# A fused agent-attention and SoLU feed-forward kernel: the same work in another order on its five queues

## The chip, the core and the metric

The kernel runs on one core of a Trainium2 chip. The core has a matrix engine (TensorE, PE in the profile; PEld is its weight load), a vector engine (VectorE, DVE), a scalar engine (ScalarE, ACT), a general engine (GpSimd, POOL) and SyncE (SP), which here does nothing but issue transfers. Each works through its own instruction stream in order; semaphores hold an instruction until what it needs is there. The metric is device time in microseconds (us) of one execution, lower is better.

## What is computed

Cut to what matters, the reference is:

```python
scale = 1.0 / np.sqrt(128)
def sm(a, b):                                   # B = 4 batches
    s = scale * (a @ b.transpose(0, 2, 1))
    e = np.exp(s - s.max(-1, keepdims=True))
    return e / (e.sum(-1, keepdims=True) + 1e-09)
agent_v = sm(agents, k) @ v                     # 49 agents, 12608 keys per batch
x = (sm(q, agents) @ agent_v).reshape(50432, 128)
h = x @ w_in                                    # 128 -> 1024
e = np.exp(h - h.max(-1, keepdims=True))
solu = h * e / (e.sum(-1, keepdims=True) + 1e-09)
ln = (solu - mean(solu)) / sqrt(var(solu) + 1e-06) * g_ln
out = ln @ w_out                                # 1024 -> 128
```

All inputs and the output are float32.

## The kernel before

The 50432 tokens are cut into 394 tiles x of 128 tokens. Three kinds of work are interleaved.

**Phase A** (`phase_a`, once per batch b) makes the batch's small matrix from K and V: 12 blocks of 1024 keys and a short last one. `kload` (L581) and `vload` (L587, and L592 for the short block's pieces) issue loads of 512 KB each; then come scores on PE (L598), maximum on DVE (L603, L610), exponential on ACT (L624), transposes on PE (L631), their copy (L641) and the product with V on PE (L651), added up on DVE (L660). Its end is a chain of small steps, among them `f1` (PE L707, the batch's agent_v), `f2` (L710, ACT copies it to `av_dup`), `q1` (DVE L714, its largest value) and the product with w_in (L741), whose result stays in SBUF as `mh` and `ml`, float16 halves. Batch 0's phase A stands at the head of the program; that of batch b+1 is spread between the tiles of batch b, and the last batch's tiles have none beside them.

**Phase B** (`phase_b`, once per unit of 8 tiles) loads q (`qload`, L841, 512 KB), makes the second softmax's weights (PE L859, DVE L865 and L870, ACT L874, casts L879 on ACT or L881 on POOL, L885) and turns them by a transfer that transposes (`b5`, L889, into `pT`).

**The tile's own steps.** PE makes h (`c_h`, L951, into `ph`, two buffers). DVE scales it and takes the extreme (`c_max`, L967, into `e_a` or `e_b`), ACT takes the exponential (`c_exp`, L974), DVE multiplies (`c_u`, L982, into `u`, six buffers), ACT squares for the variance (`c_sq`, L1003). For 343 of the 394 tiles u is split into two float16 parts (`c_f0`, L990 on POOL or L988 on ACT; `c_f1`, L993 on POOL; `f`, five buffers), and a transfer transposes both parts (`c_x`, L997 on SP, into `x`, eight buffers); the other 51 are transposed on PE (L1010). Then PE multiplies by w_out (`c_w`, L1031). Per 16 tiles the row factors are made (`c_rstd`), and per group of 4 tiles `c_fin` (DVE L1078, into `ob_a` or `ob_b`) scales the sums and `c_out` (SP L1082) stores 256 KB. `c_fin` of group g writes the buffer that the store of group g-2 reads.

**What sets the order.** The kernel lists all its steps with their dependencies (`op`), and a table of numbers, `STEPS`, gives the order in which `Plan.run` hands them out and, for steps that two engines can do, which of them does it:

```python
for i, k in todo:          # todo = steps(), unpacked from STEPS
    o = self.ops[i]
    e = o.eng[k]
```

Nothing else decides: each engine's stream, SP's among them, holds its steps in the order of this table. Steps wait for their inputs and for buffers to come free, and nothing overtakes on an engine. The times that `Plan` adds up beside this choose which of four PSUM banks a step takes, and put some filling matmuls (L1092) into PE's idle time in the head.

Of the kernel before, what the change touches and what calls it, by code (L numbers as in the profile page):

```python
# [30 lines left out]
    "B?AgPvJ2V=60J8EZT`fz$-AeSQO$h#)5lj%G<bVHZSsz{-}?4YxWFD%_l2LF10zned`jA*?$HG{o8*0-^78|qD-3!LfVD(s+yTQWr?GZ^`3w*Z"
    "jm{ZI60D4f49m%#2(}EDqnR;uXikS0g7f#78*7OguS>_`D%=H(86UnX0p$ad@rZYqs0!f|*M6n16^%59_a?T~yBZZb-ZrP~O|FgN34K(tDC^iO"
    "zgDi*D&5<=ohI*Uh01Hyt-CAHaJ(a`Jhqp4zWr4bs`3v7V<4TX(Q7T2p_PC%3glkX&;3erWqa=0dw}bWE5?;zTpp3{y2U$-y$YW`)*I`(=-LiM"
    "mcS4H)fzt9-qN1L9p{>z-oahJW9#^~Ryh`PtoCdg&XvjA=DE0|b9Z{;ZrPOFGI^&49I4?+h4|hzj9p@pW}`N!s@%5WO@m8d?qK81zCsf10+(1|"
    "Y3;nRRWj?fY4^`mD>AGaG}U{4^F#3KzotEwfW7$SB}QPW6ke+x-#Kd<U26~H$`f-P_~_e?(<(eY=EKmKucHHK_8K47@W`}1yi<J*H`0P`f92m9"
    "tv!eHmL}rV)!zn&7BdbV-qEQVw-NfmYBymDjWzeiq@vQpo3k;E-V{*Sw$O{ZgLZ%#2HV!p^kC?JkS={x8k1Xmhw{LdT|bBZ+Hcezw%MK58Tp2K"
    "#aKFF?>$@|xU)OUZ>zQSj)C!tDTlXj(BJJV)g9XJB*RjjTvq{R!HD+o&1@hvF>Nc?*GwMB?<>dg<>~dorOv9YMgO-x)q6ZIRhV{h`L$SebgC%r"
    "@n6+UG%jzYu(Q2jP!^~<nO`6}Ce$Kx<KTTl4v3@_Pn?;+&6%<qq;x*Rl7A)^x0o72RlP`M9P<f>H^W1C^lWM7&LG?G*f}4Kq8q(4<*swg{bQe%"
    "Oj~dnK<5JqFTUbg0}Ya2{<1sXC0{sJjp5S4$UYiUl%30ff2cYDErN|{<7fJS8ueSE*k1457X^nqb#EfAmA0>Z6vOt00Q?ukG!K&ag4L<}+_(2M"
    "Da*RYbkck)mV$%k+k@)%w2!bXL>CrB>5MUL-oPfo@Pd6pJd_qKDNl!8|LYgVmBZfpQ(K~9V58-5Y^(&7znM?m>lPL<Apk?Nkx)nfENXtRjaLjR"  # L40
    "S4a2jwVP7ilEgAlwbhN@RHa3-^MCPsfB2!k-zdT2LCa<1p}5gJSPe2rEHa#wnY*>|tukfBimLL`*K{_Lkj28{ChTkfFfFt9`A37Q)be<&q8y+T"
    "oh<`~3fWl$x~@Brc$$@p8I9Cy`p<vq?P@nt&H+3&7%xpd;+u+5XLDQzR`Au?Giz7{WampW4Kv=YDU011wT*ap4$oA3s<nDWxKfpB3B^_&vormx"
    "p*u<Y!mxHHT<fSGAasZ4sfrS?8gpD$40%!DP3YFm^Z)1Xnmr?P130d6bjwonolVzM3!=#>%^o2=Zob;tU*B4&@*F7=O&6>34?bCQa@I$fyTx6X"
    "m{E4Nt@GkdU>i4st&46nB6ry%n=O5WBe8gmiB6h)h7wf|s>F2RgZ5b6;V_8!>f3EDsn*#Zlh0dB>8(u_Ix+olq*`dx>>Q27#j<smx9Z|h5BEN^"
    "w|C`l^iRY;^^M(;3f&N9{ki{UK!kWZIBSSTPL}<8FgiP`MWaNbO|_qtJI7AvkLOi*2SBI9O?U!7mac+*NdTy#`U$DKcD8es7y=KD>9sy-OXzZI"
# [36 lines left out]
    "Hi2eJKJ^Wcx#`PaQwdK>M!;Ex1PH}dQH+o#amC;KIQXf5b*Q<&N8%O7-5#Ut=1L}AtrW_z_(hqr4A|`DF*ypB+Rw1Fk^a@S;lnno5jg+pUzUs7"
# [1194 lines left out]
```

## Time and profile before

| | us |
|---|---|
| Median of 3 runs | 1303.37 |
| Lowest and highest run | 1299.05 and 1303.8 |
| The profiled execution, its own time | 1300.81 |
| Span of the profiled execution (first to last instruction) | 1299.0 |

A profile gives, for one execution, when each engine was busy and what ended each idle stretch before an instruction. Read it by stage: a mean over the program mixes the head (batch 0's phase A), the long middle (tiles with the next batch's phase A beside them, to about 990 us), the last batch's tiles (990 to 1274) and the tail. A transfer has three times: when SP issues it, how long SP is held by that (the duration in SP's rows, marked SPq), and when it lands (to landing).

### The profile page before, as it was taken

The numbers are of one execution on the slowest core, as the hardware profiler recorded it, in microseconds if no ns is written. First come the engines' busy times: TensorE is split into PE (matmuls) and PEld (weight loads), VectorE is DVE, ScalarE is ACT, GpSimd is POOL, SyncE is SP. The second block draws the span as 40 slices with busy tenths as digits, with TensorE's granted clock in tenths as the row PEclk, the third lists the DMA queues.
The fourth block names the chain that finished last, engine by engine and source line by source line (L and its number), as shares of the span: only waits on it lengthen the run. The fifth ranks groups of instructions, "written<-read, shape, count | busy, mean of one in ns | idle before, by whom it ended". The sixth has DMA issues, their size and how long they took to land.

```text
span 1299.0 us, 36435 instructions
## 1 busy us (share of the span) xinstructions
PE 1204.2 (93%) x14305; PEld 916.7 (71%) x14305; DVE 1177.5 (91%) x2127; ACT 1174.8 (90%) x2157; POOL 1131.2 (87%) x910
## 2 busy tenths in 40 slices
PE   7889988999999888998989998989998999999998
PEld 4566766777777666776767776767776777776777
DVE  6899888989999888998979997988997999999997
ACT  5599888999999888998979998988997999999998
POOL 3589788899999987979988897988997999999996
PEclk9999999999999999999999999999998999999999
DMA  9699999999999999999999999999998999999988
GB/s 371 194 250 237 240 228 222 242 232 229 222 229 246 235 241 249 237 242 235 222 225 227 243 241 229 236 245 250 247 222 167 230 236 218 208 222 208 213 208 181
DMA packets 805484, 300.62 MB, mean 231 GB/s; under 512 B 770496, under 2 KB 774080, under 8 KB 805312
## 3 DMA queue, kind: packets, MB, share of 16 engines
q1 hardware_dynamic: 805312, 298.30, 108.8%
q8 instruction: 112, 1.84, 0.6%
q14 instruction: 60, 0.49, 0.1%
HBM read 79.67 MB, written 25.82 MB: 81 GB/s over the span
## 4 chain that ended last, share of the span: by engine, by line
ACT 30%; DMA 16%; PE 15%; POOL 13%; DVE 13%; issue 12%; SPq 1%; DVEq 0%; POOLq 0%; ACTq 0%
ACT ph L974 13%; ACT sq L1003 12%; PE px L1031 6%; PE ph L951 4%; DVE e_b L967 2%; POOL f_c L993 2%; POOL f_b L993 2%; DVE e_a L967 2%; POOL f_e L993 2%; DMA x_f<-f_d 2%; PE px L651 2%; DMA out_dram<-ob_a 1%; POOL f_a L993 1%; POOL f_d L993 1%; DVE u_a L982 1%
## 5 line engine op out<-in xcount | busy, mean ns | idle before, releaser
L974 ACT ACTIVATE ph<-e_a,nm 128x1024 f32<-128x1024 f32 x197 | 218.6, 1109 | 30.1 <-DVE e_a L967 28.9
L974 ACT ACTIVATE ph<-e_b,nm 128x1024 f32<-128x1024 f32 x197 | 218.5, 1109 | 14.9 <-DVE e_b L967 14.4
L951 PE MATMUL ph<-mh,pT_a 128*128 128x512 f16 x264 | 102.4, 388 | 12.5 <-DVE u_a L982 3.4
L951 PE MATMUL ph<-mh,pT_b 128*128 128x512 f16 x260 | 99.3, 382 | 13.2 <-DVE u_e L982 6.6
L951 PE MATMUL ph<-mh,pT_c 128*128 128x512 f16 x260 | 99.2, 382 | 11.0 <-DVE u_c L982 4.5
L951 PE MATMUL ph<-ml,pT_a 128*128 128x512 f16 x264 | 102.0, 387 | 0.1
L951 PE MATMUL ph<-ml,pT_b 128*128 128x512 f16 x260 | 99.4, 382 | 0.0
L951 PE MATMUL ph<-ml,pT_c 128*128 128x512 f16 x260 | 99.4, 382 | 0.0
L982 DVE SCALAR_TENSOR_TENSOR u_a<-e_a,cb,ph 128x1024 f32<-128x1024 f32 x66 | 84.2, 1276 | 5.4 <-ACT ph L974 4.4
L982 DVE SCALAR_TENSOR_TENSOR u_c<-e_a,cb,ph 128x1024 f32<-128x1024 f32 x65 | 82.9, 1275 | 4.0 <-ACT ph L974 3.3
L982 DVE SCALAR_TENSOR_TENSOR u_d<-e_b,cb,ph 128x1024 f32<-128x1024 f32 x66 | 84.2, 1276 | 2.5 <-ACT ph L974 2.1
L982 DVE SCALAR_TENSOR_TENSOR u_e<-e_a,cb,ph 128x1024 f32<-128x1024 f32 x65 | 82.9, 1275 | 2.8 <-ACT ph L974 1.8
L982 DVE SCALAR_TENSOR_TENSOR u_b<-e_b,cb,ph 128x1024 f32<-128x1024 f32 x65 | 82.8, 1274 | 2.7 <-ACT ph L974 2.2
L982 DVE SCALAR_TENSOR_TENSOR u_f<-e_b,cb,ph 128x1024 f32<-128x1024 f32 x65 | 82.9, 1275 | 2.4 <-ACT ph L974 1.6
L951 PEld LDWEIGHTS <-pT_a 128*128 128x128 f16 x528 | 47.9, 99 | 48.3 <-issue 21.1
L951 PEld LDWEIGHTS <-pT_b 128*128 128x128 f16 x520 | 47.3, 98 | 48.5 <-issue 20.5
L951 PEld LDWEIGHTS <-pT_c 128*128 128x128 f16 x520 | 46.8, 98 | 46.2 <-issue 17.6
L1031 PE MATMUL px<-wh,x_f 128*128 128x128 f16 x688 | 73.0, 221 | 5.1 <-DMA x_f<-f_d 2.2
L1031 PEld LDWEIGHTS <-x_a 128*128 128x128 f16 x1032 | 64.0, 99 | 18.9 <-DMA x_a<-f_b 3.4
L1031 PE MATMUL px<-wh,x_a 128*128 128x128 f16 x688 | 73.4, 221 | 4.0 <-DMA x_a<-f_b 2.4
L1031 PEld LDWEIGHTS <-x_f 128*128 128x128 f16 x1032 | 63.9, 99 | 18.1 <-DMA x_f<-f_d 2.4
L1031 PE MATMUL px<-wh,x_e 128*128 128x128 f16 x688 | 72.5, 219 | 3.9 <-DMA x_e<-f_c 1.3
(472 smaller groups left out, 4842.5 us busy)
## 6 DMA issues: line engine op xcount, KB each, us to landing
out_dram<-ob_a SPq DMA_DIRECT2D x49, 256.0 KB, 2.8
out_dram<-ob_b SPq DMA_DIRECT2D x49, 256.0 KB, 2.8
qt_a<-in_qT_dram SPq DMA_DIRECT2D x24, 512.0 KB, 5.1
qt_b<-in_qT_dram SPq DMA_DIRECT2D x24, 512.0 KB, 5.1
kt_b<-in_kT_dram SPq DMA_DIRECT2D x18, 512.0 KB, 5.1
vt_b<-in_v_dram SPq DMA_DIRECT2D x18, 512.0 KB, 5.8
kt_a<-in_kT_dram SPq DMA_DIRECT2D x18, 512.0 KB, 4.9
vt_a<-in_v_dram SPq DMA_DIRECT2D x18, 512.0 KB, 5.3
```

The source lines that it names most:

```text
L651: nc.tensor.matmul(px[h * AP2 : (h + 1) * AP2, :C], eT[:w, o + h * AP2 : o + (h + 1) * AP2], vt[:w, t, :], start=all(z[0] != h for z in mm ...
L951: nc.tensor.matmul(ph[:, sl], w, m[:, sl], start=(q == 0), stop=(q == len(mm) - 1))
L967: nc.vector.tensor_scalar(out=nhs[x], in0=phs[x], scalar1=nkr[k % 4][:, j : j + 1], scalar2=None, op0=ALU.mult, op1=ALU.min, accum_out=nms[x])
L974: nc.scalar.activation(out=phs[x], in_=nhs[x], func=AF.Exp, scale=-1.0, bias=nms[x], accum_out=rs_[R]["S"][:, j : j + 1])
L982: nc.vector.scalar_tensor_tensor(out=u, in0=nhs[x], scalar=scal(x)[:, 4:5], in1=phs[x], op0=ALU.mult, op1=ALU.mult, accum_out=su)
L993: nc.gpsimd.tensor_tensor(out=fs[x][:, 1, :], in0=us[x][0], in1=fs[x][:, 0, :], op=ALU.subtract)
L1003: nc.scalar.activation(out=sq, in_=u, func=AF.Square, bias=su, scale=-float(DF), accum_out=rs_[R]["Q"][:, j : j + 1])
L1031: nc.tensor.matmul(po, ut, wt[:, kf, :], start=(q == 0), stop=(q == len(mm) - 1))
```

## The change

Only the table `STEPS` differs. Steps, dependencies, buffers and transfers are the same; the order of the steps on every queue is another one, and some steps that two engines can do go to the other engine. The change is described as planning the order anew, with measured mean transfer times and with late landings told by PE's instruction number. The new orders differ from the old nearly everywhere, by a few places.

```diff
--- before.py
+++ after.py
@@ -23,129 +23,129 @@
 STEPS = (
-    "c-pOb4^V1tdf(v{y<9%y7<$T_&vmS^#!!|J<G99J$8}xGu!dU48p2xE5Mmi)EaMu+5^AlnhOmTK;~K|WYKbw_u+|u3T-UI~_!&d2>l%jevDO%C"
...
+    "c-pOb4NxoVdEV+nM~ACRC{Z`+nlPsf!CbDa%2>seU_ywZ5P~r#m=J{!LS+r5l*m+76pg|Vie;jzDv=4M3}L83RSm`rLkU(?MO9=CA><6ERF-vh"
...
 )
```

Engine choices, counted in the built programs: the cast of phase B on ACT (L879) 24 before and 19 now, on POOL (L881) 28 and 33; the small product L913 on ACT 25 and 20, L915 on POOL 29 and 34; the copy L641 on ACT 49 and 47, on DVE 3 and 5; the 1024-column cast on ACT (L988) 64 and 67, on POOL (L990) 279 and 276; four small copies on POOL (L897), two of which are now on ACT (L895). The filling matmuls L1092 are 38 and 46.

Three places of the order follow. In all three, letters count the buffers of a ring, and numbers behind a name count tiles of the program.

**SP, around tiles 242 to 244.** L997 is the transpose of a tile's two halves, L581 and L587 load K and V, L841 loads q, L1082 stores a group, L889 is phase B's transpose. Before:

```order
L1082 DMA out_dram<-ob_b 128x512
L997 DMA_TRANSPOSE x_d<-f_b 128x16x128
L997 DMA_TRANSPOSE x_e<-f_c 128x16x128
L581 DMA kt_a<-in_kT_dram 128x1024
L1082 DMA out_dram<-ob_a 128x512
L587 DMA vt_b<-in_v_dram 128x1024
L587 DMA vt_a<-in_v_dram 128x1024
L997 DMA_TRANSPOSE x_f<-f_d 128x16x128
L581 DMA kt_b<-in_kT_dram 128x1024
L997 DMA_TRANSPOSE x_g<-f_e 128x16x128
```

Now:

```order
L997 DMA_TRANSPOSE x_c<-f_a 128x16x128
L841 DMA qt_a<-in_qT_dram 128x1024
L581 DMA kt_b<-in_kT_dram 128x1024
L889 DMA_TRANSPOSE pT_b<-pack_a 128x8x128
L1082 DMA out_dram<-ob_a 128x512
L581 DMA kt_a<-in_kT_dram 128x1024
L587 DMA vt_b<-in_v_dram 128x1024
L997 DMA_TRANSPOSE x_d<-f_b 128x16x128
L997 DMA_TRANSPOSE x_e<-f_c 128x16x128
L997 DMA_TRANSPOSE x_f<-f_d 128x16x128
L997 DMA_TRANSPOSE x_g<-f_e 128x16x128
```

Four transfers stood in a row ahead of the transpose into x_f; now six stand ahead of the one into x_d, two tiles earlier, and none ahead of x_f.

**ACT, at the end of the last batch's phase A (tiles 284 to 287).** L710 copies `av_dup`, on which DVE's L714 waits; L974 and L1003 are the tiles' exponentials and squares, L988 and L1015 a cast and a copy. DVE has L714 behind the L967 of tile 287 in both orders. Before:

```order
L1015 COPY t_d<-px_169 128x512
L974 ACTIVATE ph_166,S_13131<-e_a,nm_13388 128x1024
L974 ACTIVATE ph_167,S_13131<-e_b,nm_13396 128x1024
L988 CAST f_e<-u_d 128x1024
L1003 ACTIVATE sq_13451,Q_13132<-u_d,su_f 128x1024
L1003 ACTIVATE sq_13454,Q_13132<-u_c,su_e 128x1024
L710 COPY av_dup<-px_170 128x128
L974 ACTIVATE ph_166,S_13131<-e_a,nm_13470 128x1024
```

Now:

```order
L974 ACTIVATE ph_167,S_13152<-e_b,nm_13319 128x1024
L1003 ACTIVATE sq_13368,Q_13153<-u_a,su_c 128x1024
L1003 ACTIVATE sq_13382,Q_13153<-u_c,su_e 128x1024
L1003 ACTIVATE sq_13396,Q_13153<-u_e,su_a 128x1024
L974 ACTIVATE ph_166,S_13152<-e_a,nm_13398 128x1024
L1015 COPY t_d<-px_171 128x512
L710 COPY av_dup<-px_169 128x128
L974 ACTIVATE ph_167,S_13152<-e_b,nm_13417 128x1024
```

The copy L710 stood behind the exponential of tile 287, a cast and two squares; now it stands behind the exponential of tile 286 and a copy, ahead of the exponential of tile 287.

**DVE, at the groups 30 to 32.** L1078 is `c_fin`; the third one in these rows writes `ob_a` again and waits for the store of the first. Before:

```order
L1078 TENSOR_TENSOR ob_a<-px_169,yc_6654 128x512
L1078 TENSOR_TENSOR ob_b<-px_170,yc_6654 128x512
L967 TENSOR_SCALAR e_b,nm_6777<-ph_167,nk_c 128x1024
L982 SCALAR_TENSOR_TENSOR u_a,su_c<-e_a,cb_4311,ph_166 128x1024
L603 TENSOR_REDUCE mxp_5240<-px_169 128x1
L982 SCALAR_TENSOR_TENSOR u_b,su_d<-e_b,cb_4311,ph_167 128x1024
L967 TENSOR_SCALAR e_a,nm_6845<-ph_166,nk_c 128x1024
L1078 TENSOR_TENSOR ob_a<-px_171,yc_6654 128x512
```

Now, from the same place:

```order
L1078 TENSOR_TENSOR ob_a<-px_171,yc_6665 128x512
L1078 TENSOR_TENSOR ob_b<-px_170,yc_6665 128x512
L967 TENSOR_SCALAR e_b,nm_6801<-ph_167,nk_c 128x1024
L982 SCALAR_TENSOR_TENSOR u_a,su_c<-e_a,cb_4312,ph_166 128x1024
L603 TENSOR_REDUCE mxp_5340<-px_170 128x1
L982 SCALAR_TENSOR_TENSOR u_b,su_d<-e_b,cb_4312,ph_167 128x1024
L610 TENSOR_SCALAR nmp_5341<-mxp_5340,nmp_5341 128x1
L967 TENSOR_SCALAR e_a,nm_6848<-ph_166,nk_c 128x1024
L603 TENSOR_REDUCE mxp_5340<-px_171 128x1
L967 TENSOR_SCALAR e_b,nm_6879<-ph_167,nk_c 128x1024
L982 SCALAR_TENSOR_TENSOR u_c,su_e<-e_a,cb_4312,ph_166 128x1024
L610 TENSOR_SCALAR nmp_5341<-mxp_5340,nmp_5341 128x1
```

Between the second and the third L1078 stood five instructions; now sixteen stand there, and the third comes six rows below the end of this piece.

## Rows read from the trace of the kernel before

**Rows 1.** The page, part 1: busy us of each engine (share of the span) and instructions.

```profile
PE 1204.2 (93%) x14305; PEld 916.7 (71%) x14305; DVE 1177.5 (91%) x2127; ACT 1174.8 (90%) x2157; POOL 1131.2 (87%) x910
```

**Rows 2.** Windows: stretch, us, busy us (instructions) by engine, granted clock, DMA share, GB/s.

```profile
78.00:990.00 912.00, 850.29 (x10151) 649.13 (x10150) 824.13 (x1481) 828.51 (x1527) 805.18 (x635) 0.98 1.14 235
990.00:1274.00 284.00, 268.98 (x3271) 209.87 (x3270) 277.46 (x476) 279.43 (x494) 273.60 (x211) 1.00 1.05 213
```

**Rows 3.** Line L967 (DVE): its engine sat idle before it (us, times) until:

```profile
  PE ph L951: 43.9, 55
```

**Rows 4.** Line L997 (the transposes): who waited for it (us, times), and landing.

```profile
  PE px L1031: 26.2, 30
DMA to landing us min/median/max: 3.6/4.7/11.2
```

**Rows 5.** Line L997 in 990 to 1274, where the view names nobody who waited.

```profile
DMA to landing us min/median/max: 3.6/4.2/8.0
```

**Rows 6.** Timeline of SP around 858: start us, us held, queue, line, transfer.

```profile
856.31 0.53 SPq L581 DMA_DIRECT2D kt_a<-in_kT_dram  x1
856.90 0.42 SPq L1082 DMA_DIRECT2D out_dram<-ob_a  x1
857.37 0.42 SPq L587 DMA_DIRECT2D vt_b<-in_v_dram  x1
857.89 0.43 SPq L587 DMA_DIRECT2D vt_a<-in_v_dram  x1
858.42 5.89 SPq L997 DMA_TRANSPOSE x_f<-f_d  x1
```

**Rows 7.** The chain that ended last, 858 to 870: start us, us, what.

```profile
858.42 9.48 DMA x_f<-f_d
...
868.80 1.66 PE ph L951 x4
```

**Rows 8.** Timeline of DVE at its three longest waits for PE; idle before in brackets.

```profile
293.00 1.28 DVE L967 TENSOR_SCALAR_CACHE_REDUCE e_b<-ph,nk_a 128x1024 f32<-128x1024 f32 x1 [3.86 <-PE ph L951]
...
799.54 1.28 DVE L967 TENSOR_SCALAR_CACHE_REDUCE e_a<-ph,nk_c 128x1024 f32<-128x1024 f32 x1 [6.04 <-PE ph L951]
...
870.49 1.28 DVE L967 TENSOR_SCALAR_CACHE_REDUCE e_a<-ph,nk_a 128x1024 f32<-128x1024 f32 x1 [3.06 <-PE ph L951]
```

**Rows 9.** The page, part 3: the queue of instruction loads: packets, MB, share.

```profile
q8 instruction: 112, 1.84, 0.6%
```

**Rows 10.** DMA view of 1105.7 to 1113.8: packets by queue; issue and us to landing.

```profile
q8 instruction: 1, 0.02, 0.8%
...
x_e<-f_e SPq DMA_TRANSPOSE x1, 8.0
```

**Rows 11.** DMA view of 1113.9 to 1118.0, no instruction load in it; us to landing.

```profile
x_g<-f_b SPq DMA_TRANSPOSE x1, 4.0
```

**Rows 12.** Timelines of DVE and ACT, 979 to 985, end of the last phase A.

```profile
984.34 0.29 DVE L714 TENSOR_REDUCE pk<-px 128x1 f32<-128x128 f32 x1 [4.81 <-ACT av_dup L710]
...
980.71 1.03 ACT L988 CAST f_e<-u_d 128x1024 f16<-128x1024 f32 x1
981.64 1.14 ACT L1003 ACTIVATE sq<-u_d,su_f 128x1024 bf16<-128x1024 f32 x1
...
984.06 0.24 ACT L710 COPY av_dup<-px 128x128 f32<-128x128 f32 x1
```

**Rows 13.** Timeline of DVE at the end of the phase A before that one.

```profile
657.07 0.29 DVE L714 TENSOR_REDUCE pk<-px 128x1 f32<-128x128 f32 x1 [1.32 <-ACT av_dup L710]
```

**Rows 14.** Timeline of DVE: four `c_fin` that waited for a store.

```profile
208.74 0.69 DVE L1078 TENSOR_TENSOR ob_a<-px,yc 128x512 f32<-128x512 f32 x1 [4.52 <-DMA out_dram<-ob_a]
...
508.62 0.69 DVE L1078 TENSOR_TENSOR ob_a<-px,yc 128x512 f32<-128x512 f32 x1 [3.52 <-DMA out_dram<-ob_a]
...
669.46 0.69 DVE L1078 TENSOR_TENSOR ob_a<-px,yc 128x512 f32<-128x512 f32 x1 [3.36 <-DMA out_dram<-ob_a]
...
886.25 0.69 DVE L1078 TENSOR_TENSOR ob_b<-px,yc 128x512 f32<-128x512 f32 x1 [2.15 <-DMA out_dram<-ob_b]
```

More of the change, by code (lines that the diff above doesn't have):

```diff
@@ L31 @@
[L31 to L45, printed above, removed]
@@ L146 @@
[L146 to L148 removed]
+    "c-pOb4NxoVdEV+nM~ACRC{Z`+nlPsf!CbDa%2>seU_ywZ5P~r#m=J{!LS+r5l*m+76pg|Vie;jzDv=4M3}L83RSm`rLkU(?MO9=CA><6ERF-vh"
+    "DJ6suWrG!&5)OwSvD<HdB<)JLai$qStaiWse%|kWpXYtvPkGppl#Pt(qf+_O-lfXk&=&%i$|I>FwcdQJI;>ZoHZH#!81LIqg;YUwcKf<avZ-2c"
@@ new lines @@
+    "J5sMnMv`E&SF)iTcb8e^^OI89qPaeFsaZ!sW%8zUrLXjaXuNJ)SEjD7DsBCVj_XKwuvog^5%F3guh8wu$YD?NX1c2MqUoX^wd?A89djk{Q`{lh"
+    "+VI!zR$5gjLkA5z7scAwHI?oQ_kL-x?`+<(Q`(bC*6x&UDYS+Ow9H#u?b7Zvp#z@XMN{3S!4s2%pt{eQTpugnYX&`AqI7rltWenQ9atNm8zoL9"
+    "Xi5(7<ay;KCc)yVYHataQ69licm2`8rD91p(=El^SUDlZoY$kWq-4CuBNkq*U@=10Qj;*rv3@5O-KjrJRP6oEdnt#_)rcP&v8c?viS!PlnAugb"
+    "jmt4v>f4_S|Kyj){``+z%Qtc?sP<Hh#`cE&o_f7$C8V0H83coy#mXZOY7csy0pH@3>7Re?wz4NR)?i%_Z8Q{P8}31SqB1Zh)i(_4K{SZlqG0y$"
+    "_~6wtZo9Pjj%s4-1Hbit$If7FGp53&MsQYj<nCFLn-bUK7>bp489k1Vem8{v(obq@)5=&?kEOF?O;+hY8?oC#yMMZVXYe>uRaKo@!1vZtgI>4a"
@@ new lines @@
+    "o5DOUuW0w&wOZchM2T{Z^2mf<$3{|TSL&n6MN32-N5A!jc1IlPv)4QKfKxQqk+Nd;&f48mE&e;7>zg}wg>lW$>a0?=Ha6KhI{#ar?+s%9y~&Wi"
+    "bl;*Mz-8d0Uy53Fa)Wf}^~lHm``};yP*1mIv&pNQv4Y#gj0;6mXNhJTrbRnzXNO7#BugW&CLE^WqxRcb%fj{b;C4^h>e(wzWu#VuhAS)go3<DH"
+    "b0K5bX;KnLx+bkBHT$)oUE+-D&SD8?tmb5@Ejr?>j#>i&C0YfxiJlWI)_A1|j{U*^(dZ6^rT%$Lrf8T7M`n(fW<%rAV0C@}n)GOG05k3=i(R#$"
+    "sOu2SZbx;vx6*}n?Z{)7a`4~Iem#Y^%mue}X1oQ6rvr0`>bNZ6-Vvv5LlKv|?56a%7OanIEj3}&>$U!P^SlZSL_#u;+HH*9>HL_!vv*<a7%L0+"
+    "0MMqx%N1>_L&+PgM6{)|TKbkA%EyRF5t@>MiOc5IgQVo<x4)oEZ_Z)*2{5H5TJ`9Z{$WY49X?1@jO}+`yn65-OoMG{T}5ZdP|1PJF!AcPWXtQW"
@@ new lines @@
+    "m>C-I6({hdUTdzN=t$$Q0NCg&OH_DOcOpetc3BLTv_JA)bgeP{@am!XpkZm`RKNakeBOzwmKuaaM1HCK>ZeXyary4S(JC631ve`@-Ri)h57_Nt"
+    ")IGQ{8OMxmYV=B@9F#3tn)i-zM@6l)z6K=w)psLWlj<_krk;~)oYi2{c5sc?qFPte{xL2m;#-wA$KWNVOt;S8ouD1fD+^<-%Qe?65i}{i>-HbF"
+    "tu}9(G&WGR*SoAuElwsMijSkclKtlMk^aC68ftOfA_E@x{zCtXc&cY(Qh!yO1mG{eX1H5STc@Xwl#|ZU#iUhtFcleEoxJwihQ=p4mBr48OQKw|"
+    "DkN76$thsD3gS^?#q8*MPw?mdvS%<^KC*t*_vas9x=Yrj$Cg0LVM@KbRVOdDn&hFD)7rC#JMrSqAO6ES%k-^JaeH{D_cou@_rF@6X>N@mA(d(F"
+    "+SgsaSkY95&J8ByXw<n9J!(kUeOtn=xXTb#)E-M?GalDCG=;xCyzMfMjC;eaChWo)M+x_gqe`BX6OK+fKH~y&<LHnMtLZ7T`1)gV$IR7=2=i=R"
@@ L149 @@
+    ")RB1"
 )
```

212 lines of the change are left out of this document (105 added, 107 removed).

## The prediction, made before the changed kernel ran

> **What bounds the kernel now.** I read the page's busy times first [rows 1]: no engine is full, and four lie within 73 us of each other, PE, DVE, ACT and POOL, all between 1131.2 and 1204.2 us of a span of 1299.0. Such a mean hides stages, so next come the windows [rows 2]. In 990 to 1274, where no phase A runs, DVE is busy 277.46 of 284 us (97.7%), ACT 279.43 and POOL 273.60: that stage is full, and no order makes it shorter. In 78 to 990 DVE is busy 824.13 of 912 us (90.4%), so 88 us are idle there. Were it as full as the last stage, it would last 824.13/0.977 = 843.6 us; 68 us are the most that an order could bring. The next view is what ended DVE's idle time. Its dearest entry is L967, waiting for the h tile of PE's L951: 43.9 us in 55 waits [rows 3]. PE in turn waits for the transposes of L997: 26.2 us in 30 times [rows 4], and none of it lies in 990 to 1274 [rows 5]. The landings differ there: the slowest of the program takes 11.2 us, that of the last stage 8.0.
>
> The timeline of SP and the chain of waits, read at 858, show how one goes to the other. Four transfers of K, V and output go out ahead of the transpose into x_f [rows 6]. It lands 9.48 us after its issue, not the median 4.7 [rows 4, 7]; PE stands until then, makes L1031 and then the h tile, and DVE starts at 870.49 after 3.06 us of waiting [rows 7, 8]. Direct transfers ahead of a transpose on SP make it late: of the 15 transposes with four or more others since the one before, 13 landed over 7 us after issue (rows 7 have one); of the 191 with none between, no one did. A second pattern follows PE's instruction number. The program loads its instructions in 112 pieces of 16 KB [rows 9], some 255 PE instructions apart, and a transpose in flight beside one landed after 8.0 us, one shortly after it, with none beside it, after 4.0 [rows 10, 11].
>
> **The change, part by part.** The sum is made against the profiled execution, 1300.81 us (span 1299.0, 1.8 around it); the median of the runs is 1303.37, 2.6 above it, and the forecast is shifted by that.
>
> *Engine choices.* Five casts of phase B, five small products and three 1024-column casts or so change engine; each is one instruction, the wide cast 1.03 us on ACT [rows 12]. Three of these more on ACT are +3.1, and the small ones that leave it give that back; against 1174.8 and 1131.2 us of busy time this is nothing by itself [rows 1]. Taken at 0; bounds -3 and +3, three wide casts either way. The head and tail keep their steps, with some neighbours swapped; no row prices that. Taken at 0 too, with one wait of the size of rows 8, 4 us, either way for the range.
>
> *End of phase A.* DVE's L714 waits for ACT's copy L710. At the last batch DVE stood 4.81 us, since ACT had a cast and two squares ahead of the copy [rows 12]. Now L710 stands behind the exponential of tile 286 and a copy, ahead of that of tile 287. I take 0.8 of waiting to be left, so -4.0 (its far end -4.8). At the end of the phase A before that the wait was 1.32 [rows 13]; there L710 now stands behind two squares, a cast and an exponential, while DVE has two tile instructions to do meanwhile: the same four on ACT are some 4.4 us at 1.03 to 1.14 each, DVE's two some 2.5 at 1.28, so 2 to 2.5 us of waiting, +1.0. The first boundary: 0. Together **-3.0**, bounds -4.8 and +1.
>
> *Stores.* `c_fin` writes the buffer that the store of two groups earlier reads, and four times it waited long [rows 14]. Of these, the one at 508.62 (3.52 us) has now sixteen DVE instructions ahead of it where it had five, and the one at 886.25 (2.15) has 16 us of DVE's work where it had 11: both go, -5.7. Those at 208.74 and 669.46 keep the same tight order or a tighter one: they stay. Two others (groups 28 and 52) come closer, from 11.9 and 8.5 us of DVE's work to 5.0, about as close as the four that waited. I put them together at half of what the four cost on the mean (3.39 each), +3. Net **-2.7**, bounds -5.7 (no new wait) and +5 (both wait in full, and one old one stays).
>
> *Late transposes.* This is the largest term. What tells is how many other transfers stand on SP between two transposes. At the 6.04 us wait, 799.54 [rows 8], the transposes that PE awaited (tiles 222 to 227) had three and four ahead; now none and one: -6.0. At the 3.86 us wait (tile 62) five stood ahead and now one at most, with three ahead of tile 60: half of it, -1.9. At 3.06 (tiles 242 to 244) the crowd of four gives place to one of six, two tiles earlier: 0. Against this the new order has more crowds: 40 transposes with three or more transfers ahead where there were 33, of these 19 with four or more where there were 15. All 43.9 us of L967's waits [rows 3], put on 33 crowds, are 1.3 each; seven more are +9 at most. I take +4, since not all those waits come from crowds, and transposes with nothing ahead went from 191 to 209. Net **-3.9**. Bounds: if nearly all of PE's 26.2 us go [rows 4], less the +4, -22; if four of the seven cost what the three of rows 8 do on the mean, 4.3, +17.
>
> The load of instructions follows PE's number, which an order can count ahead. I found no more cover for the transposes in the new order on the whole: between a transpose's issue and its first use PE has about the same work, a little less. So no gain is added for that.
>
> Here a rule of the Trainium skill bears: the page "Runtime: NRT & Kernel Launch", section "Instruction fetch mechanics", says that a block of instructions is refilled by 16 KiB, that crossing costs one DMA bump and that straight-line code hides most of it. The loads' size agrees with the trace, 1.84 MB in 112 [rows 9]; that it is hidden does not hold for a transpose in flight, 8.0 against 4.0 us [rows 10, 11]. If it were hidden, knowing PE's number would bring nothing, which is one reason for the first rival below.
>
> The sum: 0 - 3.0 - 2.7 - 3.9 = **-9.6**; 1300.8 - 9.6 = 1291.2 for a profiled execution, 1303.4 - 9.6 = **1293.8** for the median.
>
> **Rivals.** *The late landings fall elsewhere* (about the same). Transfers and bytes are the same, and counts of crowds are like before. If each old wait is replaced by a new one as long, the last term is 0 and -3.0 - 2.7 = -5.7 are left: 1297.7; if the stores and the copy are covered by other waits too, 1303. For it: the waits are many and short (55 for 43.9 us), so that two places are a small part [rows 3]. Here belongs also that the change does not do what it says: the order counts PE's instructions, fillers included (38 and now 46), and late landings shift as soon as one wait comes out otherwise.
>
> *More crowds, more waits* (slower). Mechanism: K, V and q loads issued in rows, up to seven together, ahead of a transpose that PE needs at once, as at 858 [rows 6, 7]. Four of the seven added crowds at 4.3 us are +17; with the -5.7 that is +11.3: 1314.7. It decides from three such places on, if no old wait goes (3 x 4.3 = 13, less 5.7, +7). For it: 33 and 40; the six in a row at tile 243. Against: a row of direct transfers sent together leaves the transposes behind it free, and those with none ahead rose by 18.
>
> *The waits really go* (much faster): crowds now stand only where x is ahead by several tiles, so PE's waits for transposes, 26.2 us, nearly all go [rows 4]: -22 and the half of -5.7, since DVE then comes sooner to the stores, -25 in all at the most, and some 1281 when ACT and POOL, at 828.51 and 805.18 of 912 us, begin to be waited for [rows 2].
>
> **How the numbers follow.** Forecast .38, late landings elsewhere .28, more crowds .22, waits really go .12. About 0.5% (6.5 us) is what a measurement of this kernel can tell from no change, so faster means under 1296.9, slower over 1309.9. Faster: .31 of the forecast's .38, all of .12, .03 of the first rival: .46. Slower: .18 of the crowds' .22, .04 of the first rival, .02 of the forecast: .24. Left: .30. The forecast's own range is 1286 to 1300; to hold 8 in 10 it must take in most of the two ends: 1278 to 1316.
>
> **What would show it.** In the profile of the changed kernel: L714's wait at the last end of phase A under 1.5 us, at the one before about 2; no `c_fin` wait at groups 32 and 61; no wait of DVE over 3 us at tiles 222 to 227; L967's waits for PE between 30 and 45 us; the window behind 990 within 2 us of 284, all change lying before it. Wrong would be: a stage before 990 that is longer while L714's and the stores' waits went (then the crowds decide, and PE's waits for L997 exceed 26.2 us), or L967's waits under 25 (then the order does hide the landings, and I have overlooked how).

## The result, and the profile after

The changed kernel takes **1291.46 us**, the median of 5 runs (1288.25 to 1293.5), against 1303.37 for 5 runs of the kernel before: a ratio of 0.9916, with a 95% interval of 0.9889 to 0.9942. The forecast was 1293.8. The profiled execution has a span of 1286.5 us, 12.5 less than that of before; it was the fastest of the five, 3.2 us under their median, as the profiled one of before lay 2.6 under its own.

The page's busy times and the windows, to be held against [rows 1, 2]:

```profile
PE 1192.2 (93%) x14313; PEld 908.2 (71%) x14313; DVE 1175.9 (91%) x2129; ACT 1173.4 (91%) x2150; POOL 1129.7 (88%) x915
```

```profile
78.00:990.00 912.00, 851.56 (x10307) 650.15 (x10306) 838.32 (x1512) 836.45 (x1537) 812.44 (x648) 1.00 1.15 237
990.00:1274.00 284.00, 267.91 (x3274) 209.21 (x3272) 274.44 (x466) 280.61 (x495) 275.87 (x213) 1.00 1.08 215
```

The work is the same: DVE is busy 1175.9 us where it was 1177.5. Its idle time fell from 1299.0 - 1177.5 = 121.5 to 1286.5 - 1175.9 = 110.6 us, by 10.9, and that is nearly the whole 12.5. In 78 to 990 DVE is now busy 838.32 of 912 us, 91.9% instead of 90.4%. The last stage begins some 12 us sooner now, so its own window is 978 to 1261: it is as full as before (97.1%, where it was 97.7%). So the gain lies where the forecast had it, ahead of the last batch's tiles.

```profile
978.00:1261.00 283.00, 267.08 (x3257) 207.03 (x3255) 274.74 (x475) 279.17 (x494) 276.19 (x214) 1.00 1.08 215
```

What ended DVE's idle time in the changed kernel: ahead of L967, of L982, of L1078 and of L714 (one fence for each line's view; us, times).

```profile
  PE ph L951: 29.5, 27
```

```profile
  ACT ph L974: 20.3, 51
```

```profile
  DMA out_dram<-ob_a: 11.3, 8
  PE px L1031: 3.1, 2
  POOL yc L1069: 1.8, 3
  DMA out_dram<-ob_b: 1.3, 1
```

```profile
  ACT av_dup L710: 4.0, 4
```

Of before, L967's entry is in [rows 3]; those of L982, L1078 and L714 were:

```profile
  ACT ph L974: 15.5, 47
```

```profile
  DMA out_dram<-ob_a: 11.9, 4
  DMA out_dram<-ob_b: 2.2, 1
```

```profile
  ACT av_dup L710: 7.1, 3
```

L967's waits for PE fell from 43.9 to 29.5 us. The waits for ACT ahead of L982 rose, from 15.5 to 20.3. The stores cost 12.6 where they cost 14.0. L714's waits for the copy are 4.0 where they were 7.1. The transposes land as before, only their extremes moved a little [rows 4]; PE waits as long for them, 26.5 us against 26.2:

```profile
  PE px L1031: 26.5, 25
DMA to landing us min/median/max: 3.6/4.7/11.6
```

The four sums (-14.4, +4.8, -1.4, -3.1) are those of one execution each, and the runs below show how far one execution goes astray. The starts of L982 (`c_u`, DVE) of some tiles, read from the trace of every run, cut the program in pieces that can be compared between orders:

| us from tile to tile | 0 to 260 | 260 to 280 | 280 to 300 | 300 to 393 |
|---|---|---|---|---|
| before | 842.7 | 60.1 | 66.4 | 258.3 |
| after | 833.5 | 63.6 | 60.0 | 259.6 |

Two pieces gain, 9.2 and 6.4 us, and two lose, 3.5 and 1.3 (the head and the tail, not in the table, give 0.8 us each). The end of the last phase A lies in the third. The experiments ask which of this is lasting, and what makes it.

### The profile page after: what moved, and what is told of

Read it like the earlier page. It is cut to its first block, busy times and chain, and to the rows that moved or that the text cites. A ratio compares the mean times of both kernels' runs of the same rounds, so it can differ in the third digit from the quotient of the medians.

```text
span 1286.5 us, 36503 instructions
## 1 busy us (share of the span) xinstructions
PE 1192.2 (93%) x14313; PEld 908.2 (71%) x14313; DVE 1175.9 (91%) x2129; ACT 1173.4 (91%) x2150; POOL 1129.7 (88%) x915
## 4 chain that ended last, share of the span: by engine, by line
ACT 27%; DMA 19%; POOL 16%; issue 14%; DVE 12%; PE 10%; SPq 1%; DVEq 0%; POOLq 0%; ACTq 0%
ACT ph L974 12%; ACT sq L1003 11%; PE px L1031 4%; DVE e_a L967 3%; POOL f_d L993 2%; DVE e_b L967 2%; DMA x_b<-f_c 2%; POOL f_b L993 2%; DMA x_e<-f_c 2%; PE ph L951 2%; DMA out_dram<-ob_a 2%; POOL f_e L993 2%; POOL f_c L993 2%; POOL f_a L993 1%; DMA x_d<-f_b 1%
## 5 line engine op out<-in xcount | busy, mean ns | idle before, releaser
L974 ACT ACTIVATE ph<-e_a,nm 128x1024 f32<-128x1024 f32 x197 | 218.7, 1110 | 27.5 <-DVE e_a L967 26.4
L974 ACT ACTIVATE ph<-e_b,nm 128x1024 f32<-128x1024 f32 x197 | 218.6, 1110 | 18.7 <-DVE e_b L967 17.9
L951 PE MATMUL ph<-mh,pT_a 128*128 128x512 f16 x264 | 99.9, 378 | 13.4 <-DVE u_a L982 4.1
L951 PE MATMUL ph<-mh,pT_b 128*128 128x512 f16 x260 | 98.3, 378 | 13.8 <-DVE u_c L982 3.6
L951 PE MATMUL ph<-mh,pT_c 128*128 128x512 f16 x260 | 98.4, 378 | 6.5 <-DVE u_e L982 2.6
L951 PE MATMUL ph<-ml,pT_a 128*128 128x512 f16 x264 | 99.9, 378 | 0.0
L951 PE MATMUL ph<-ml,pT_c 128*128 128x512 f16 x260 | 98.4, 378 | 0.0
L951 PE MATMUL ph<-ml,pT_b 128*128 128x512 f16 x260 | 98.4, 378 | 0.0
L982 DVE SCALAR_TENSOR_TENSOR u_e<-e_a,cb,ph 128x1024 f32<-128x1024 f32 x65 | 82.9, 1276 | 6.2 <-ACT ph L974 5.0
L982 DVE SCALAR_TENSOR_TENSOR u_a<-e_a,cb,ph 128x1024 f32<-128x1024 f32 x66 | 84.2, 1276 | 4.4 <-ACT ph L974 3.7
L982 DVE SCALAR_TENSOR_TENSOR u_f<-e_b,cb,ph 128x1024 f32<-128x1024 f32 x65 | 82.9, 1275 | 5.1 <-ACT ph L974 4.5
L982 DVE SCALAR_TENSOR_TENSOR u_d<-e_b,cb,ph 128x1024 f32<-128x1024 f32 x66 | 84.1, 1274 | 2.2 <-ACT ph L974 1.9
L982 DVE SCALAR_TENSOR_TENSOR u_b<-e_b,cb,ph 128x1024 f32<-128x1024 f32 x65 | 82.9, 1275 | 3.1 <-ACT ph L974 2.8
L982 DVE SCALAR_TENSOR_TENSOR u_c<-e_a,cb,ph 128x1024 f32<-128x1024 f32 x65 | 82.8, 1274 | 3.0 <-ACT ph L974 2.3
L951 PEld LDWEIGHTS <-pT_b 128*128 128x128 f16 x520 | 47.5, 97 | 52.9 <-issue 22.9
L951 PEld LDWEIGHTS <-pT_a 128*128 128x128 f16 x528 | 47.6, 97 | 50.7 <-issue 20.6
L1031 PE MATMUL px<-wh,x_b 128*128 128x128 f16 x688 | 74.3, 220 | 7.8 <-DMA x_b<-f_c 4.6
L1031 PE MATMUL px<-wh,x_e 128*128 128x128 f16 x688 | 72.7, 219 | 7.7 <-DMA x_e<-f_c 3.8
L1031 PEld LDWEIGHTS <-x_b 128*128 128x128 f16 x1032 | 64.4, 99 | 21.7 <-DMA x_b<-f_c 5.1
L1031 PEld LDWEIGHTS <-x_e 128*128 128x128 f16 x1032 | 63.0, 98 | 20.1 <-DMA x_e<-f_c 4.9
L1031 PE MATMUL px<-wh,x_f 128*128 128x128 f16 x688 | 71.3, 219 | 5.1 <-DMA x_f<-f_d 2.5
L951 PEld LDWEIGHTS <-pT_c 128*128 128x128 f16 x520 | 46.9, 97 | 40.8 <-issue 10.9
```

What stands on the lines that cost most here:

```text
L951: nc.tensor.matmul(ph[:, sl], w, m[:, sl], start=(q == 0), stop=(q == len(mm) - 1))
L974: nc.scalar.activation(out=phs[x], in_=nhs[x], func=AF.Exp, scale=-1.0, bias=nms[x], accum_out=rs_[R]["S"][:, j : j + 1])
L982: nc.vector.scalar_tensor_tensor(out=u, in0=nhs[x], scalar=scal(x)[:, 4:5], in1=phs[x], op0=ALU.mult, op1=ALU.mult, accum_out=su)
L1031: nc.tensor.matmul(po, ut, wt[:, kf, :], start=(q == 0), stop=(q == len(mm) - 1))
```

## The experiments

Three theories. **One place**: the copy L710 at the end of the last phase A. **Crowds**: transfers no longer stand in rows ahead of a transpose that PE needs at once. **Number**: the order has PE work ready just where a load of instructions delays a transpose, and so depends on PE's instruction numbers; against it stands **place**, that these do not matter. Each ran beside the kernel before on the same chip, and each ratio is to its runs there. Their medians were 1301.25 us (beside e1 to e4), 1301.08 (e5 to e8) and 1300.0 (e9 to e12). The changed kernel itself did not run there again, so it is compared by its ratio.

### PE's numbers shifted

In the changed kernel (and once in that of before), tiny matmuls in PE's first idle time raise the number of every later PE instruction; nothing changes place.

```diff
                 nc.tensor.matmul(ph2[1][:, : 2 * P], warm[:, :P], warm, start=True, stop=True)
+            if plan.at["P"] <= 2.0:
+                for _ in range(64):
+                    nc.tensor.matmul(ph2[1][:8, :8], warm[:, :8], warm[:, :8], start=True, stop=True)
```

> The changed kernel with 64 tiny filling matmuls (8 columns, 128 PE instructions with their weight loads) at the head, in PE's idle time before the first keys land (5.8 us in the changed kernel). Every later PE instruction keeps its place in the order and gets a number higher by 128, half of the distance between two instruction loads. If the gain comes from where transfers and steps stand (place), the time stays at the changed kernel's, 1288 to 1295 us, and DVE's waits for the h tile near 29.5 us. If the order gains because it has PE work ready at the transposes that a load of instructions delays (number), the late ones now fall on other transposes: DVE's waits for h rise by half or more of the 14.4 us by which they fell, to 37 to 45 us, and the time to 1297 to 1304 us.

> The kernel before with the same 64 tiny matmuls at the head (PE's idle time there is 4.3 us). Place expects 1299 to 1306 us, DVE's waits for h 40 to 48 us. Number expects the same if the old order knew nothing of the loads, and a slower time by some us if the old order was fitted to them as well: above 1307 us.

> The changed kernel with 128 tiny matmuls at the head, 256 PE instructions, a full distance between two instruction loads: the loads fall beside the same instructions as in the changed kernel. Number expects the changed kernel's time, 1288 to 1295 us, plus at most 2 us for the longer filling of the head (128 at some 57 ns are 7.3 us, of which 5.8 us lie in PE's idle time); DVE's waits for h near 29.5 us. Place expects the same. A time near 1300 us here would say that it is the filling itself that costs, and not the numbers.

The two other shifts came in the last group, to see whether one shift had been lucky:

> The changed kernel with 32 tiny matmuls at the head: a quarter of the distance between two instruction loads. With the shift by 128 the time was 1294.64 us, with 256 (none, in effect) 1293.46, unshifted 1291.46. If PE's number doesn't matter (place), 1291 to 1295 us and DVE's waits for h 27 to 36 us; if the order was fitted to it (number), 1296 us or more with the waits above 36 us in this run and in the next one.

> The changed kernel with 96 tiny matmuls at the head, three quarters of the distance. Place: 1291 to 1295 us, DVE's waits for h 27 to 36 us. Number: 1296 us or more, waits above 36 us.

| | shift | median us | ratio to before, 95% | L967's waits for PE | tile 0 to 260 |
|---|---|---|---|---|---|
| after | 0 | 1291.46 | 0.9916 (0.9889 to 0.9942) | 29.5 | 833.5 |
| e3 | 256 | 1293.46 | 0.9951 (0.9927 to 0.9975) | 27.2 | 829.5 |
| e11 | 64 | 1290.95 | 0.9930 (0.9905 to 0.9954) | 36.9 | 841.1 |
| e1 | 128 | 1294.64 | 0.9943 (0.9924 to 0.9963) | 35.7 | 840.8 |
| e12 | 192 | 1297.92 | 0.9987 (0.9964 to 1.0009) | 29.1 | 836.6 |
| e2, old order | 128 | 1303.41 | 1.0009 (0.9984 to 1.0034) | 35.7 | 837.1 |

The old order does not mind. For the new one, neither theory has it whole. With shifts by 64 and 128 the interval overlaps that of the unshifted kernel, as place expects. The shift by 192 loses most of the gain, as number expects, though its waits at L967 are low and its interval overlaps e3's. With the shift by 256 the loads do fall as planned: 314 of the 343 transposes have a load near their start, or none, as in the unshifted kernel (149 to 194 at the other shifts). The traces seem to lean to number: the piece from tile 0 to 260 takes 833.5 and 829.5 us where the loads fall as planned (839.7 in e7 below, which has that piece too), and 841.1, 840.8 and 836.6 where they don't. That is some 5 us on the mean, against 843.0 for the six profiles of the old order here and below. But the two lowest figures come from executions that were the fastest of their kernel, 3.2 and 5.3 us under the median, and e11's 841.1 from the slowest of its seven, 7.3 over the median, in a kernel whose median is the lowest of the table. So one profile of each can't settle it. The pieces from 280 on are alike at each shift. The order keeps a gain without its numbers, and in two of three shifts the whole time is as good; how much the numbers are worth stays open between 0 and 6 us.

L967's own waits are a poor witness: 43.9 and 35.7 in two profiles of the old order, 27.2 to 36.9 in five of the new one. The means are 39.8 and 31.7: of the -14.4 above some 8 last, and the rest is the chance of one execution.

### The transfers' order alone

The kernel before, with SP's queue from the new table and every other queue as it was (the fillings as well):

```diff
-        todo = steps()
+        todo = self.merge(steps(STEPS), steps(STEPS_NEW), "S")
...
-                idle(s - self.at[e])
+                idle(self.FILL.get(i, 0))
```

> The kernel before, with its order on PE, DVE, ACT and POOL, its engine choices and its 38 filling matmuls, and with SP's order of the changed kernel. If the order of the transfers by itself brings the gain, 1290 to 1296 us. If crowds on SP and the compute order are fitted to each other, transfers now come at places where the old order does not cover them: 1303 us or more, with PE's waits for transposes above the 26.2 us of before.

It takes 1395.1 us (ratio 1.0718, 1.0685 to 1.0752): 94 us slower, far past what was expected. Its waits, of L967, of L1078 and of PE for the transposes (lines are shifted by what was added to the file: L1116 and L1100 are L967 and L951, L1180 is L1031):

```profile
  PE ph L1100: 81.4, 67
```

```profile
  DMA out_dram<-ob_a: 25.4, 6
  DMA out_dram<-ob_b: 14.4, 5
```

```profile
  PE px L1180: 53.8, 32
```

L967's waits nearly doubled (43.9 before), PE's for the transposes doubled (26.2) and those for stores nearly trebled (14.0), with not one instruction of a computing engine moved. PE's idle time rose from 88 to 160 us, and a transfer that landed ended 57 of the 71 us more. One thing beside SP's order changed, though: `Plan`'s times choose which of four PSUM banks PE writes a product to, and in the built program 7855 of PE's 12583 matrix instructions go to another bank than before. What that costs was not tested. PE's waits that neither a transfer nor a u tile ended, those for a bank among them, rose by 7 us, so the transfers' order is the likely cause of most of the 94. SP's order is then no better or worse by itself: SP's stream is worked in order and each transfer waits for its source, so one that stands too early holds up all that stand behind it. Counting crowds in it, as the prediction did, says little.

### The copy alone

The kernel before with L710 of the last phase A ahead of the exponential of tile 287 on ACT. On ACT's queue:

```diff
+L710 COPY av_dup<-px
 L974 ACTIVATE ph_167<-e_b       (tile 287)
 L988 CAST f_e<-u_d
 L1003 ACTIVATE sq<-u_d
 L1003 ACTIVATE sq<-u_c
-L710 COPY av_dup<-px
```

> The kernel before with one step moved on one engine: at the end of the last phase A the copy L710 stands ahead of the exponential of tile 287 on ACT, where it stood behind it, a cast and two squares. All else is the old order. In the old order DVE takes 66.4 and 70.4 us (two profiles) from tile 280 to tile 300, in the new one 60.0, 59.9 and 60.0 (three). If this place is the main part of the gain (one place), that stretch comes down to 60 to 63 us, L714's wait of 4.81 us goes to under 1 us, the wait of 1.70 us behind it goes as well, and the time falls by 4 to 7 us, to 1294 to 1297. If the gain is spread over the many moved steps (spread), L714's wait is taken over by another one, the stretch keeps 64 us or more, and the time falls by 2 us at most, to 1299 or more.

1295.9 us, ratio 0.9959 (0.9935 to 0.9983): 5.2 us less than before on that chip, with one instruction moved. DVE's and ACT's timelines there (L718, L714 and L978 are L714, L710 and L974 of the old numbering), against [rows 12]:

```profile
981.90 0.29 DVE L718 TENSOR_REDUCE pk<-px 128x1 f32<-128x128 f32 x1 [0.26 <-ACT av_dup L714]
```

```profile
980.47 1.12 ACT L978 ACTIVATE ph<-e_a,nm 128x1024 f32<-128x1024 f32 x1 [0.80 <-DVE e_a L971]
...
981.62 0.24 ACT L714 COPY av_dup<-px 128x128 f32<-128x128 f32 x1
981.76 1.12 ACT L978 ACTIVATE ph<-e_b,nm 128x1024 f32<-128x1024 f32 x1
```

The wait of 4.81 us is 0.26, and the piece from tile 280 to 300 takes 59.4 us instead of 66.4. The piece gains more than the wait. In the old order PE stood too, 4.63 us, for the u tile that DVE makes behind L714, and then worked at half its clock; a first h tile's matmuls took 0.63 us instead of 0.38, and DVE waited 1.70 us more for the next h tile, at 990.77. PE's and DVE's timelines of before, and its windows (the granted clock is the last figure but two), then a window of the copy alone:

```profile
985.88 0.58 PE L951 MATMUL ph<-mh,pT_b 128*128 128x512 f16 x1 [4.63 <-DVE u_e L982]
986.26 0.63 PE L951 MATMUL ph<-ml,pT_b 128*128 128x512 f16 x1
```

```profile
990.77 1.28 DVE L967 TENSOR_SCALAR_CACHE_REDUCE e_b<-ph,nk_b 128x1024 f32<-128x1024 f32 x1 [1.70 <-PE ph L951]
```

```profile
985.00:991.50 6.50, 5.62 (x19) 3.71 (x19) 4.65 (x8) 1.24 (x2) 2.96 (x3) 0.50 0.53 118
991.50:996.00 4.50, 4.50 (x66) 3.45 (x65) 4.30 (x11) 3.44 (x6) 1.59 (x2) 0.99 0.28 50
```

```profile
982.00:988.00 6.00, 5.93 (x72) 4.86 (x69) 6.00 (x11) 5.90 (x10) 5.87 (x6) 1.00 1.15 265
```

PE, that waits for nothing long now, keeps the full clock, and the second wait is gone with the first. In every profile here the piece from 280 to 300 takes 59.4 to 60.5 us with the copy moved, and 65.8 to 70.5 without. One place is shown, for this much: the 5.2 us have an interval of 2.2 to 8.5.

### Half of one order, half of the other

Up to tile 262 by one table, the rest by the other; the end of the last phase A is in the second half.

(`C_U_262` stands for the number of that step.)

```diff
-        todo = steps()
+        todo = steps(STEPS)
+        todo = todo[: [i for i, _ in todo].index(C_U_262) + 1]
+        done = {i for i, _ in todo}
+        todo += [z for z in steps(STEPS_2) if z[0] not in done]
```

> The order of before up to tile 262 (some 905 us), then the changed one: the rest of the program, with the end of the last phase A in it, in the new order. One place expects nearly all of the gain, 1293 to 1297 us; spread expects a gain in proportion to the tiles, a third, 1298 to 1300 us.

> The changed order up to tile 262, then that of before, the reverse of the run ahead of this one. One place expects little gain, 1297 to 1301 us, and 4.8 us of waiting at L714 of the last end; spread expects two thirds of the gain, 1294 to 1297 us.

1301.47 us (ratio 1.0003, 0.9986 to 1.0020) and 1303.36 (1.0019, 1.0003 to 1.0035): no gain in either, which neither theory expected. The pieces:

| us from tile to tile | 0 to 260 | 260 to 280 | 280 to 300 | 300 to 393 |
|---|---|---|---|---|
| e5, copy alone | 844.5 | 60.0 | 59.4 | 258.5 |
| e6, old then new | 846.8 | 65.2 | 59.9 | 258.1 |
| e7, new then old | 839.7 | 64.0 | 66.3 | 259.5 |

The piece with the copy is as each order has it, 59.9 and 66.3, so one place holds again. But e6 loses at the seam most of what it gains there, 65.2 us for 260 to 280 where the old order has 60.1. The new order itself takes 63.6 in this piece, e7 64.0 at its seam. As a division of the gain these two runs are inconclusive.

### Crowds thinned, alone and with the copy

The kernel before with three crowds on SP taken apart; at tiles 222 and 223 this is

```diff
-L841 DMA qt_b<-in_qT_dram
-L587 DMA vt_a<-in_v_dram
-L1082 DMA out_dram<-ob_b
 L997 DMA_TRANSPOSE x_c<-f_e
+L1082 DMA out_dram<-ob_b
+L587 DMA vt_a<-in_v_dram
 L997 DMA_TRANSPOSE x_d<-f_a
+L841 DMA qt_b<-in_qT_dram
```

and likewise two V loads go behind the transpose of tile 244, a q and a V load behind that of tile 62.

> The kernel before with three crowds on SP thinned and nothing else moved: three transfers now behind the transposes of tiles 222 and 223 instead of ahead of both, two V loads behind that of tile 244, a q and a V load behind that of tile 62. In four profiles of the old order DVE waits there (for PE's h tile) for 4.6 to 6.6 us at tile 226 in each, 2.2 to 3.1 us in three of the four at some 870 us, 2.3 to 3.9 us in three of the four at some 290 us. If the crowds make these waits (crowds), they go and nothing as long comes for them: 5 to 10 us less than before, 1291 to 1296 us. If a late landing is only passed on to the next transposes (passed on), DVE waits as long within the next six tiles, and the time is that of before, 1299 to 1303 us.

> The kernel before with the three thinned crowds and the copy L710 moved as in the run of the copy alone, which took 5.2 us off. Crowds expects both to add up: 1287 to 1291 us, as fast as the changed kernel or faster, with eight steps moved. Passed on expects the copy's gain alone, 1294 to 1298 us.

Alone: 1302.79 us (ratio 1.0019, 1.0002 to 1.0036), nothing gained. With the copy: 1294.43 (0.9941, 0.9920 to 0.9961), 5.6 us less than before, about the copy's 5.2; against the thinned crowds alone the copy is worth 8.4 us here. DVE's timeline of e9 at the second and third place (L971 and L955 are L967 and L951 of the old numbering, L664 is L660):

```profile
802.69 1.28 DVE L971 TENSOR_SCALAR_CACHE_REDUCE e_a<-ph,nk_c 128x1024 f32<-128x1024 f32 x1 [3.09 <-PE ph L955]
...
824.06 1.28 DVE L971 TENSOR_SCALAR_CACHE_REDUCE e_a<-ph,nk_c 128x1024 f32<-128x1024 f32 x1 [3.32 <-PE ph L955]
...
871.90 0.35 DVE L664 SCALAR_TENSOR_TENSOR av<-av,fc_g,px 128x128 f32<-128x128 f32 x1 [4.97 <-PE px L655]
...
876.88 1.28 DVE L971 TENSOR_SCALAR_CACHE_REDUCE e_a<-ph,nk_a 128x1024 f32<-128x1024 f32 x1 [1.63 <-PE ph L955]
```

The wait of some 6 us, in fact at tile 230, is down to 3.09, and 3.32 us come 21 us behind it; at the third place the wait for h is 1.63 us where it was 3.06, but L660 waits 4.97 us for PE ahead of it. At the first place DVE still waits 2.93 us (3.86 before). Passed on holds, and PE's waits show the way of it: at 870 PE stood 3.89 us for a V load that had been put behind the transpose, and at the first place 3.16 us for the transpose that follows the one that was freed. The transfers that left one transpose's way came late themselves, or made the next one late.

### Five more moves in the changed kernel

L710 of the third phase A ahead of a square and an exponential, and three stores ahead of one or two transfers each, where DVE waited for them.

```diff
+        for i, j, d in [(3616, 3288, 0), (3672, 3686, 1), (3907, 3934, 1), (4512, 4182, 1), (5216, 4512, 1)]:
+            n = [z for z, _ in todo]
+            t = todo.pop(n.index(i))
+            todo.insert([z for z, _ in todo].index(j) + d, t)
```

> The changed kernel with five steps moved: at the end of the third phase A the copy L710 ahead of a square and an exponential of ACT (DVE waits 1.86 us for it in the profiles), and three stores on SP ahead of one or two transfers each (DVE waits 1.73, 2.88 and 1.95 us for them at 709, 762 and 815 us). If these waits go and nothing comes late instead, 6 to 8 us less than the changed kernel, 1285 to 1288 us; if the transposes that now go out 0.5 to 1 us later or the waits behind them take half of it back, 1288 to 1291; if such waits are merely exchanged, the changed kernel's time, 1291 to 1294. In each case DVE's L714 there waits under 0.5 us.

1293.76 us, ratio 0.9940 (0.9917 to 0.9964): the changed kernel's time. L714's waits are 2.2 us in 3 where they were 4.0 in 4, and the stores' 5.8 and 2.7 where they were 11.3 and 1.3, but L967 waits 42.3 us for PE where it waited 29.5 (in these fences L714, L1035 and L955 are L710, L1031 and L951 of the old numbering):

```profile
  ACT av_dup L714: 2.2, 3
```

```profile
  DMA out_dram<-ob_a: 5.8, 8
  PE px L1035: 3.1, 2
  DMA out_dram<-ob_b: 2.7, 3
```

```profile
  PE ph L955: 42.3, 40
```

This is what merely exchanged expects; which wait came for which is not shown, since L967's sum varies that much by itself. No run here is clearly faster than the changed kernel.

## Why the prediction was right, and where it was not

The forecast of 1293.8 is 2.3 us from the median, and the gain of 11.9 stands beside a sum of 9.6. That the total came so near is in part luck: one term was too small, one too large, and the largest had a wrong mechanism. The gain is also not known to the microsecond: with its loads as planned again (e3) the new order was 7.8 us under the median of before. By the terms:

**The copy, -3.0.** Right in mechanism, too small in size. L714's waits went from 7.1 to 4.0, the 3.0 of the sum, with 0.82 us left at the last end (0.8 was taken) and 1.86 at the one before it (2.3 was taken). But the last end's move alone, for which the sum had 4.0, is worth 5.2 us, and 6.4 us in its piece of the program: the sum priced DVE's wait and not what followed from it, PE's own 4.63 us of standing, the half clock behind that and a second wait of DVE. The clock at 985 lay in the trace of before and stands in no row of the prediction.

**The stores, -2.7.** The two waits that were to go went (none at groups 32 and 61), and new short ones came at others. The two groups that the sum named for this, 28 and 52, cost 0.67 and 2.88 us, as it had them together (+3); it did not name the others, such as 1.73 us at 709 and 1.95 at 815. Of the two that were to stay, the one at 208.74 fell from 4.52 to 1.47 and that at 669.46 is gone. From 14.0 to 12.6 us it is -1.4 in the two profiles.

**Late transposes, -3.9.** The size came out near what is left of the gain, by luck: the step that gave it does not hold. It took single crowds by the waits that they made, -6.0 at tiles 222 to 227 and -1.9 at tile 62, and charged the places to which the transfers go by the number of crowds alone, +4. One of these readings was wrong besides: of the two crowds at the 6.04 us wait, the four ahead of tile 227's transpose went out at 800 to 802 us, behind the wait's end at 799.54; PE had stood for the transposes of tiles 222 and 223. Thinning these crowds in the old order gave 0 (e9), and the new SP queue in the old kernel costs 94 us (e4). In the new order this wait is gone, and in the same profile one of 6.39 us stands at 733:

```profile
733.00 1.28 DVE L967 TENSOR_SCALAR_CACHE_REDUCE e_b<-ph,nk_d 128x1024 f32<-128x1024 f32 x1 [6.39 <-PE ph L951]
```

In those of e1, e3, e11 and e12 it is 0.8 to 1.3 us, in that of e8 4.26. What the new order does gain between tiles 0 and 260, 9.2 us in the two profiles and 3.5 to 9 on the means, can't be put down to single places from these runs. The transfers' order alone does not give it (e4); the computing order alone was not run, so that both are needed together is not shown.

**No gain for PE's number.** The prediction found no more cover for the transposes and added nothing. By the shifts, 0 to 6 us may hang on the numbers: this is open, and whether the zero was right is not known.

**What it missed:** 260 to 280 costs 3 us more on the mean in the profiles of the new order (62.9 to 66.6 against 60.0 to 62.9 in five of the old one without a seam). The larger gains elsewhere hid that.

**The rivals.** That late landings fall elsewhere (.28) describes the waits well: PE waits for the transposes 26.5 us as before, at other places, and 40 transposes land over 7 us after issue in both traces. That more crowds make more waits did not come: 40 crowds of three or more instead of 33, and no slower. The count of crowds did not decide the time here. Of the signs named, one just failed: L967's waits, 29.5 us, lie under the 30 to 45 that were expected; but the sum varies by more than that from one execution to the next.

## What to carry to other kernels

In a kernel whose engines are all nine tenths full, look first for a small step of a serial chain that stands in a queue behind work nobody waits for, above all where PE comes to stand for it and then works at half its clock: one copy put ahead of one exponential gave 5.2 us, where the whole new order gave 11.9 (7.8 in e3). Don't price a queue's order by one engine's waits or by counts on that queue: the same order of transfers stands in the faster kernel with the computing order that it was made for, and cost 94 us with another (other PSUM banks came with it). And before a sum of waits is called a gain, read it in a second execution: one such sum went from 43.9 to 35.7 us with nothing but PE's numbers changed, and the time stayed.

## What the runs showed of the hardware

A load of PE's instructions holds the data transfers up. In the DMA view of before from 793 to 798, in which one load of 16 KB began at 794.3, the rate falls to nothing for a time (40 slices of 0.125 us, GB/s):

```profile
GB/s 291 289 293 287 293 285 295 291 289 287 372 262 272 260 39 0 0 0 0 0 0 0 0 0 8 6 10 10 8 10 117 289 291 287 257 281 270 274 289 256
```

Fifteen slices, 1.9 us, are at 10 GB/s or less. It is no single case: on the mean of the 104 loads between 80 and 1270 us, where a transfer was under way, the rate goes from some 270 GB/s ahead of a load to some 60 from 0.75 to 1.6 us behind its start. The same transpose with and without a load beside it, in the changed kernel (155 to 160) and in e11 (162 to 166), by their DMA views:

```profile
q8 instruction: 1, 0.02, 1.1%
...
x_g<-f_c SPq DMA_TRANSPOSE x1, 5.1
```

```profile
x_g<-f_c SPq DMA_TRANSPOSE x1, 4.0
```

The five profiles of the new order (e1, e3, e11, e12 and the changed kernel) have the same 343 transposes with the loads at other places (in e3 nearly where the changed kernel has them). 302 of them had a load near their start (from 1 us ahead of it to 3 us behind) in some profiles and none in others. For the 189 with no other transfer between them and the transpose ahead, it made the landing later by 0.94 us on the mean (standard error 0.04), for the 82 with one or two by 0.46 (0.09), and for the 31 with three or more by 0.03 (0.20): behind a crowd no cost is seen. So [rows 10, 11] were over-read: the transpose of rows 10 had a q load just ahead of it, and among the 82 like it a load made 1.8 us at the most, not the 4.0 between these two rows. By these means an order that knows its loads has about one microsecond to win at each, where that is not covered; this is an estimate. The Trainium skill (page "Runtime: NRT & Kernel Launch", section "Instruction fetch mechanics") calls the cost of crossing a 16 KiB boundary mostly hidden. It speaks of the engine that fetches; that a transfer in flight pays these 0.94 us is beside that rule and not against it.

PE's clock adds to a long wait, and not only at the copy. In before PE was busy 1.52 of 4 us while it waited for the transposes of tiles 222 and 223, and in the 4 us behind that the granted clock was 0.57, nearly all at the lower of its levels of 1.2 and 2.4 GHz (windows, columns as in [rows 2]):

```profile
793.00:797.00 4.00, 1.52 (x25) 1.36 (x26) 0.51 (x2) 2.37 (x5) 1.71 (x2) 1.00 1.16 143
797.00:801.00 4.00, 4.00 (x20) 2.08 (x20) 1.29 (x2) 0.13 (x1) 3.14 (x2) 0.57 1.16 259
```

The h tile that DVE awaited for 6.04 us [rows 8] was made at that clock. The prediction counted it nowhere.
